# Last pair of a long convolution with spectral mixing: early loads of Z split in two parts and spread over ticks 9 to 14, and two VectorE reflections placed behind the last product

## The chip, the core and the metric

The kernel runs on one core of one Trainium2 chip. A core has a matrix engine (TensorE, PE in the profile; its weight loads are listed as PEld), VectorE (DVE), ScalarE (ACT), GpSimd (POOL) and SyncE (SP), and 16 DMA engines that they share. The metric is the device time of one execution in microseconds (us); the number compared is the median of several runs.

## What is computed

Two steps, one after the other, on x of 8 batches by 5696 positions by 128 channels. The first is a causal convolution of each channel with a filter h as long as the sequence. The second takes the first 64 Fourier modes of that result, mixes the channels of each mode with a complex 128 by 128 matrix, transforms back, adds this to the first result and ends with a dense layer.

```python
Xf = rfft(x, n=2*S, axis=1); Hf = rfft(h, n=2*S, axis=0)
x = irfft(Xf * Hf, n=2*S, axis=1)[:, :S, :]          # long convolution
X = rfft(x, axis=1); Xr, Xi = X[:, :64].real, X[:, :64].imag
Yr = einsum('bmd,mde->bme', Xr, w_r) - einsum('bmd,mde->bme', Xi, w_i)
Yi = einsum('bmd,mde->bme', Xr, w_i) + einsum('bmd,mde->bme', Xi, w_r)
u = x + irfft(Y, n=S, axis=1)                         # Y is zero beyond mode 64
out = u + maximum(u @ w_ch, 0)
```

Everything between the inputs and the output is in float16, with sums in float32.

## The kernel before

**Tiling.** The 5696 positions are split as 89 by 64, so the long transforms become matrix products with constant matrices: F1, M (read in 90 frequency groups k, "As, M" in the profile), W1 and W2. The batches are handled in four pairs (g_ = 0 to 3). For each pair there is a phase that makes As from x (`a_tile`, "F, Xin"), and then a loop of ticks: the 90 groups are cut into 23 ticks of four (the last has two).

**One tick.** `tick(g_, t)` issues, for tick t: `second`, 16 TensorE matmuls of As with M into PSUM; then `products`, which multiplies by the filter's spectrum on VectorE ("U<-Xs,Hs", or "U<-ps,Hs" in every fourth tick, straight from PSUM), in most ticks after ScalarE has copied PSUM to Xs (`copied`). For tick t - 2 it issues `third`: four matmuls of U with W1 and W2, two evacuations by ScalarE into a buffer Zs or Zt, and one store by SP from that buffer to the scratch `zscr` in HBM. For tick t - 3 it issues `modes_of`: eight small matmuls with G that add up the 64 modes in PSUM bank 7. The buffers Zs0 to Zs4 and Zt0 to Zt3 are used in turn; in the last pair there are eight of them (`NZS`), so tick s + 8 writes where tick s has been, and `third(s + 8)` can't start its evacuation before the store of tick s has landed. All ScalarE evacuations and copies stand in one program order.

**After the ticks of the last pair.** The 64 modes of the pair are evacuated to XT in two instructions, the first on ScalarE, the second ("xtn", the negated part) on VectorE behind it, as both read one bank. `mix` multiplies XT with the mode matrices W, `y_out` evacuates that to Y, eight transposes and two evacuations make C. Then the output stage: for each of the 16 chunks of Z (4 pairs by 4 chunks), `u_tile` adds up matmuls of Z with the constants S4a and S4b, which transform back, and of C with the constant IBs, and evacuates to UT on VectorE or ScalarE; `o_tile` applies the dense layer and stores to the output. In both kernels the first U tile's matmuls with Z stand ahead of `mix` on TensorE, and other tiles' stand between the parts of `mix`.

**Loads of the output stage.** A chunk of Z is read back from `zscr` into one of five places ZT0 to ZT4, each in two parts: part a with 128 rows of 8 KB (1024 KB), part b with 52 rows (416 KB) in partitions 32 to 83; partitions 0 to 31 of part b are cleared by a GpSimd memset (`clear_zt`). The places lie on memory that is still in use during the last pair's ticks: ZT2 on the first rows of the filter's spectrum (Hs), ZT0 and ZT1 on the middle and late part of As, S4b on its first part, IBs and S4a on M. So each load waits for the last reader of what it overwrites (`zt_old`). The constants IBs (734.2 KB), S4a (734.2 KB) and S4b (481.9 KB) hold only the first half of their columns; the rest, 2759 columns, is filled by `reflect` (L525), which writes the mirrored columns times a sign per row: S4b on ScalarE (L530), S4a and IBs on VectorE (L532).

**The order around the change** is written out by hand. The dictionary `early` (L540 to 543) says at which tick of the last pair which load is issued. They are issued by GpSimd, whose queue is in order: a waiting load or clear holds up those behind it. `pace` makes each wait for the product of its own tick t on VectorE. In this kernel the order is S4b at tick 6, IBs at 8, both parts of ZT2 at 10, clear of ZT2b at 11, clear of ZT0b at 14, both parts of ZT0 at 15, S4a at 16, ZT1 at 21 (`NT - 2`; this one also waits for the last pair's stores up to tick 14, `SLACK`). Behind the ticks follow WI, ZT3 and ZT4. The later chunks are loaded by SP. VectorE's order behind the ticks is: the last product, "xtn", the reflection of S4a, two Y evacuations, one C evacuation, the reflection of IBs, UT evacuations.

Semaphore waits are derived by a recorder from what each instruction reads and writes; all tiles' instructions are recorded through helpers, so most lines of the profile show L325 (matmul), L313, L315, L317, L319 (evacuations), L322 (DMA) and L611 (products).

Of the kernel before, what the change touches and what calls it, by code (L numbers as in the profile page):

```python
# [4 lines left out]
P = 128  # L5
# [118 lines left out]
def bass_long_conv_fft__then__afno_spectral_mix_kernel(nc, x, h, moe_w_r, moe_w_i, moe_w_ch, out):  # L124
# [8 lines left out]
    NP = B // 2  # L133
# [24 lines left out]
    s4 = np.stack([back[:, None, None] * np.cos(ang), -back[:, None, None] * np.sin(ang)], axis=0)  # L158
    RB, PB = 2 * NK - P, 32
# [13 lines left out]
    ib = modes.copy()  # L173
    ib[:, 0] *= 0.5
    ib = ib.T.reshape(2, M, NQ, J).transpose(1, 0, 3, 2).reshape(P, J, NQ)
# [30 lines left out]
    def at(name, cols, dt, off):  # L206
        return nc.alloc_sbuf_tensor_at(name, [P, cols], dt, offset=off)
# [58 lines left out]
    ib_sb = at("IBs", S, F16, a_mi)  # L266
    s4_sb = [at("S4a", S, F16, a_mi + 2 * S), at("S4b", S, F16, a_as)]
# [26 lines left out]
    def pv(bank, off, dims, p0=0, n=P):  # L294
        return bass.AP(ps, p0 * 4096 + bank * 512 + off, [[4096, n]] + [list(d) for d in dims])
# [5 lines left out]
    def bank(i):  # L301
        return ("bank", i)
# [3 lines left out]
    def evac(dst, src, reads, writes, scale=None, eng=None, after=()):  # L306
        e = eng
        if e is None:
            turn[0] ^= 1
            e = "scalar" if turn[0] else "vector"  # L310
        if e == "scalar":
            if scale is None:
                R.add(e, lambda h_: h_.copy(dst, src), reads, writes, after=after)  # L313
            else:
                R.add(e, lambda h_: h_.activation(dst, src, COPY, scale=scale), reads, writes, after=after)  # L315
        elif scale is None:
            R.add(e, lambda h_: h_.tensor_copy(dst, src), reads, writes, after=after)  # L317
        else:
            R.add(e, lambda h_: h_.tensor_scalar_mul(dst, src, scale), reads, writes, after=after)  # L319

    def dma(eng, dst, src, ring, reads=(), writes=(), after=()):
        R.add(eng, lambda h_: h_.dma_start(dst, src), reads, writes, ring=ring, after=after)  # L322
# [6 lines left out]
    def once(key, toks):  # L329
        if key in first:  # L330
            return []
        first[key] = 1
        return list(toks)
# [77 lines left out]
    def idle(n, b0, m=P):  # L411
        for i in range(n):
            mm(pv(b0 + i % 2, 0, [[2 * NK, 2], [1, 2 * NK]], 0, m), f1_sb[:, 0:m], ap(f1_sb, 2 * NK, 0, P, 0, [[0, 2], [1, 2 * NK]]),
               True, True, [("f1",)], [bank(b0 + i % 2)])
# [7 lines left out]
    for j in range(16):  # L422
        t = turns("h", [0, 2, 4])
        for i in range(8):
            d = 8 * j + i
            for r in range(2):
# [6 lines left out]
             eng="vector" if j % 4 == 1 else "scalar")  # L433
# [6 lines left out]
    def share(n):  # L440
        a, v = load["scalar"] + COST[n][0], load["vector"] + COST[n][1]
        e = "scalar" if a <= v else "vector"
        load[e] = min(a, v)
        return e
# [42 lines left out]
    def load_g(i):  # L487
        s0, s1 = i * GP, min(i * GP + GP, NS)
        dma("sync", g_sb[:, s0 * P:s1 * P], bass.AP(c_g, s0 * P, [[GW, P], [1, (s1 - s0) * P]]), "c", (),
            [("g", i)], after=[("ag", k) for k in range(s0, s1)])  # L490
# [3 lines left out]
    def load_w(i):  # L494
        w = 2 * M * D // NWP
        h_ = i % 2
        dma("gpsimd", w_sb[i // 2][:, h_ * w:(h_ + 1) * w], bass.AP(wd, i * w, [[2 * M * D, P], [1, w]]), "p",
            [t_ for t_ in WD if (t_[1] * M + t_[2]) * D // w == i], [("w", i)], after=[("xc", i // 2)] + pace)
# [4 lines left out]
    M_ALL = [("m", i) for i in range(MP)]  # L503
# [3 lines left out]
    ZX = [("zs", i, b) for i in range(NZ, NZL) for b in range(2)]  # L507
    zt_old = [(AST, AST), (AST, AST), (H_ALL, H_ALL), (H_ALL, H_ALL), (M_ALL[3:6], G_ALL)]

    def load_zt(i, eng="sync", more=()):  # L510
        g_, c_ = divmod(i, J // ZB)
        for part, (p0, r0, n) in enumerate(((0, 0, P), (PB, P, RB))):
            old = list(once(("zt", i % NC, part), zt_old[i % NC][part])) + list(more) + pace
            dma(eng, bass.AP(zt[i % NC][part], p0 * ZP, [[ZP, n], [1, ZP]]),
                bass.AP(zs, (g_ * 2 * NK + r0) * J * 256 + c_ * ZB * 256, [[J * 256, n], [1, ZP]]),
                "q" if eng == "gpsimd" else "t", [("zd", g_, s_) for s_ in range(NT)], [("zt", i % NC, part)], after=old)

    def clear_zt(i):
        z32 = zt[i][1][0:PB, :].bitcast(U32)
        R.add("gpsimd", lambda e: e.memset(z32, 0), (), [("zt0", i)], after=list(zt_old[i][1]) + pace)  # L520

    def load_ib():
        dma("gpsimd", ib_sb[:, 0:SH], c_ib.ap(), "p", (), [("ib", 0)], after=M_ALL[0:2] + pace)

    def reflect(eng, t, n, col, key, after):  # L525
        MN = S - SH
        dst, src = bass.AP(t, SH, [[S, n], [1, MN]]), bass.AP(t, SH - NQ - 1, [[S, n], [-1, MN]])
        sc = sg_sb[0:n, col:col + 1]
        if eng == "scalar":
            R.add(eng, lambda e: e.activation(dst, src, COPY, scale=sc), [key + (0,), ("sg",)], [key + (1,)], after=after)  # L530
        else:
            R.add(eng, lambda e: e.tensor_scalar_mul(dst, src, sc), [key + (0,), ("sg",)], [key + (1,)], after=after)  # L532

    def load_s4(part):
        n = PB + RB if part else P
        dma("gpsimd", s4_sb[part][0:n, 0:SH], bass.AP(c_s4, part * SH, [[2 * SH, n], [1, SH]]), "p", (),
            [("s4", part, 0)], after=pace + (AST if part else M_ALL[1:4]))

    V, A = "vector", "scalar"
    early = {0: lambda: (load_w(6), load_w(7), load_id()),  # L540
             6: lambda: load_s4(1), 8: lambda: load_ib(), 10: lambda: load_zt(2, "gpsimd"), 11: lambda: clear_zt(2),
             14: lambda: clear_zt(0), 15: lambda: load_zt(0, "gpsimd"), 16: lambda: load_s4(0),
             NT - 2: lambda: (load_zt(1, "gpsimd", SLACK), clear_zt(1))}
    w_at = {11: (0, 1), 17: (2, 3), 25: (4, 5)}
    pace = []
    SLACK = [("zd", NP - 1, s_) for s_ in range(NT - NZL)]

    def load_id():
        dma("gpsimd", id_sb[:, :], bass.AP(c_w, 2 * P, [[3 * P, P], [1, P]]), "p", (), [("id",)], after=ZY)
# [135 lines left out]
    for g_ in range(NP):  # L685
        for t in range(NT + LM if g_ + 1 == NP else NT):
            if g_ == 0 and t % 2 == 0 and t // 2 < NG:
                load_g(t // 2)
            tick(g_, t)
            assert g_ + 1 < NP or not wp  # L690
            if g_ == NP - 1 and t in early:
                pace[:] = [("u", min(t, NT - 1) % NU)] if t else []
                early[t]()
        if g_ + 1 < NP:
            load.update(scalar=600.0, vector=0.0)
            third(g_, NT - 2)
            a_tile(0, [0], share(720))
            a_tile(1, [2], share(720))
            third(g_, NT - 1)
            load["scalar"] += 560.0  # L700
            a_tile(2, [0], share(720))
            modes_of(g_, NT - 3)
            a_tile(3, [4], share(720))
            modes_of(g_, NT - 2)
            a_tile(4, [2], share(720))
            modes_of(g_, NT - 1)
            load["scalar"] += 700.0
        evac(bass.AP(xt, 6 * g_ + 2, [[B * XTW, P], [3 * B, M], [2, 2], [1, 2]]), pv(MB, 0, [[1, M], [M, 2], [P, 2]]),
             [bank(MB)], [("xt", g_)], 1.0 / 64, eng="scalar", after=[("ag", k) for k in range(NS + 2 * XN, NK)])
        evac(bass.AP(xt, 6 * g_, [[B * XTW, P], [3 * B, M], [1, 2]]), pv(MB, M, [[1, M], [P, 2]]),  # L710
             [bank(MB)], [("xtn", g_)], -1.0 / 64, eng="vector" if g_ + 1 == NP else "scalar", after=[("ag", k) for k in range(NS + 2 * XN, NK)])
        if g_ + 1 < NP:
            for j in range(5, 32):
                a_tile(j, [(0, 4, 6, 2)[(j - 5) % 4]], "both" if j == 31 else share(720))
                if j == 31:
                    idle(4, 2)
                if wp and j % 2 == 1:
                    dst, src_, ring, tok = wp.pop(0)
                    dma("gpsimd", dst, src_, ring, (), [tok], after=[("as", j)])
                if g_ + 2 == NP:  # L720
                    for i in w_at.get(j, ()):
                        load_w(i)
# [54 lines left out]
             src, [bank(t), bank(t + 1)], [("u_", ub, 2 * c_ + half)], eng=e, after=once(("u", ub), old))  # L777

    XTT = [(n, g_) for g_ in range(NP) for n in ("xt", "xtn")]
    reflect("vector", s4_sb[0], P, 0, ("s4", 0), M_ALL[1:4])  # L780
    reflect("scalar", s4_sb[1], PB + RB, 1, ("s4", 1), AST)
    MQ = M // 4

# [25 lines left out]
    for hb in range(2):  # L809
        evac(c_sb[:, hb * 512:hb * 512 + 512], ps16[:, (6 + hb) * 1024:(6 + hb) * 1024 + 512], [bank(6 + hb)],  # L810
             [("c", hb)], 2.0 * 64 / S, eng="vector" if hb else "scalar", after=WT)
    reflect("vector", ib_sb, P, 2, ("ib",), M_ALL[0:3])


    n_o = [0]
# [52 lines left out]
    for g_ in range(NP):  # L868
        last = g_ == NP - 1
        order = [(c_, b) for b in range(2) for c_ in range(NCH)] if last else [(c_, b) for c_ in range(NCH) for b in range(2)]  # L870
        for n, (c_, b) in enumerate(order):
            i = NCH * g_ + c_
# [44 lines left out]
```

## Time and profile before

| | |
|---|---|
| time, median of 3 runs | 379.2 us (378.95 to 379.32) |
| the profiled execution | 380.74 us, its span 378.9 us |
| PE busy | 358.8 us (95%) |
| ACT busy | 311.2 us (82%) |
| DVE busy | 302.5 us (80%) |
| POOL busy | 83.7 us (22%) |
| mean granted TensorE clock | 0.991 |
| DMA packets | 84560, 103.92 MB, mean 274 GB/s |
| chain that ended last | PE 76%, ACT 11%, DVE 7%, DMA 4% |
| reflection of S4a, of IBs (VectorE, 128x2759) | 2157 ns, 1811 ns |

All times of the trace are counted from the start of the span. The last pair's products run from 213.7 to 252.0 us. A row of a timeline gives the start, the length, the engine, the line, the operation with its output and inputs, how many instructions are merged in it, and in brackets the idle time of the engine before it and what ended that. A row of waits gives who waited for whom, the total in us, the number of times and the longest. In the DMA view, q0 ("software_dynamic") holds what GpSimd issues and q1 ("hardware_dynamic") what SP issues; the time to landing of a DMA is counted from its issue. Matmuls are pipelined and their ends modelled, so a busy PE is not PE at its peak.

### The profile page before, as it was taken

The page shows a single profiled execution, that of the slowest core. Times are in us where ns is not written, and L with a number is a line of the kernel's source. Part 1 is how long each engine was busy: PE and PEld are TensorE (multiplying, and loading weights), DVE is VectorE, ACT ScalarE, POOL GpSimd, SP SyncE. Part 2 cuts the span into 40 slices and gives each one's busy share as a digit, 9 for nine tenths or more (in the row PEclk, how much of TensorE's full clock was granted, in tenths as well). Part 3 has the DMA queues.
Part 4 walks back from the last instruction along what each step waited for, and adds up shares of the span by engine and source line. Part 5 has one row for each costly group of instructions (what it writes and reads, how often), then busy time and mean ns, then how long its engine had stood idle before and what let it go on. Part 6 is the DMA issues. An engine that isn't in the chain of part 4 may idle for free.

```text
span 378.9 us, 11952 instructions
## 1 busy us (share of the span) xinstructions
PE 358.8 (95%) x5107; PEld 275.4 (73%) x5107; DVE 302.5 (80%) x332; ACT 311.2 (82%) x493; POOL 83.7 (22%) x137
## 2 busy tenths in 40 slices
PE   7998989999989999899999899979999999999994
PEld 3897856667856667766668666648898988988872
DVE  7557998998989998889998888754547767777786
ACT  8358989998989998999998899975457677777785
POOL 8500012320932312823305303309000000000000
PEclk9999999999999999999999999998999999999998
DMA  7999599998999996999997989999999999999768
GB/s 138 209 278 349 142 233 231 273 276 233 116 133 234 254 256 162 144 153 238 256 258 122 340 262 290 290 301 331 396 410 365 354 414 406 419 408 379 301 267 348
DMA packets 84560, 103.92 MB, mean 274 GB/s; under 512 B 22126, under 2 KB 68974, under 8 KB 81538
## 3 DMA queue, kind: packets, MB, share of 16 engines
q1 hardware_dynamic: 59643, 67.73, 52.1%
q0 software_dynamic: 24864, 35.43, 44.6%
q8 instruction: 40, 0.66, 0.7%
q14 instruction: 13, 0.11, 0.1%
HBM read 70.61 MB, written 51.12 MB: 321 GB/s over the span
## 4 chain that ended last, share of the span: by engine, by line
PE 76%; ACT 11%; DVE 7%; DMA 4%; issue 1%; DVEq 0%; ACTq 0%
PE ps L325 76%; ACT As L315 7%; DMA zscr<-Zt 4%; DVE As L319 3%; DVE U L603 1%; ACT R L851 1%; ACT UT L313 1%; DVE Hs L317 1%; DVE UT L317 1%; DMA F<-cF 1%; DVE IBs L532 0%; ACT XT L315 0%; DVE O L852 0%; ACT Hs L313 0%; DVE Os L852 0%
## 5 line engine op out<-in xcount | busy, mean ns | idle before, releaser
L325 PE MATMUL ps<-U,Wc 128*128 128x512 f16 (+1 forms) x368 | 94.5, 376 | 2.5 <-ACT Zt L313 2.5
L611 DVE TENSOR_TENSOR U<-Xs,Hs 128x2048 f16<-128x2048 f16 (+1 forms) x68 | 80.5, 1188 | 10.8 <-ACT Xs L313 8.8
L313 ACT CAST Xs<-ps 128x1024 f16<-128x1024 f32 (+1 forms) x72 | 69.5, 971 | 7.0 <-PE ps L325 4.8
L852 DVE TENSOR_TENSOR O<-ps,R 128x512 f32<-128x512 f32 x81 | 52.5, 684 | 19.6 <-ACT R L851 11.2
L313 ACT CAST Zs<-ps 128x512 f16<-128x512 f32 (+1 forms) x120 | 62.9, 603 | 0.0
L851 ACT ACTIVATE R<-ps 128x512 f32<-128x512 f32 x96 | 50.9, 572 | 14.3 <-PE ps L325 13.9
L319 DVE TENSOR_SCALAR As<-ps 128x720 f16<-128x720 f32 (+1 forms) x60 | 49.8, 878 | 7.6 <-PE ps L325 6.7
L315 ACT ACTIVATE As<-ps 128x720 f16<-128x720 f32 (+1 forms) x72 | 51.0, 765 | 5.4 <-PE ps L325 4.4
L325 PE MATMUL ps<-F,Xin 128*128 128x180 f16 x512 | 52.3, 247 | 2.9 <-ACT Ah L315 1.0
L325 PE MATMUL ps<-As,M 64*128 64x128 f16 x1440 | 48.7, 217 | 4.2 <-DVE U L603 3.5
L325 PE MATMUL ps<-WI,UT 128*128 128x256 f16 x360 | 51.8, 279 | 0.5 <-DVE O L852 0.4
L325 PEld LDWEIGHTS ps<-F,Xin 128*128 128x128 f16 x512 | 43.3, 142 | 10.8 <-DVE As L319 3.9
L325 PEld LDWEIGHTS ps<-U,Wc 128*128 128x128 f16 x368 | 28.2, 97 | 31.4 <-ACT Zs L313 5.9
L325 PEld LDWEIGHTS ps<-As,M 64*128 64x128 f16 x1440 | 40.3, 94 | 10.8 <-DVE U L603 4.2
L322 POOL DMA_DIRECT2D Xt<-in_x_dram x48 | 24.9, 522 | 100.8 <-PE ps L325 100.2
L611 DVE TENSOR_TENSOR U<-ps,Hs 128x2048 f16<-128x2048 f32 x20 | 45.7, 2283 | 0.0
L313 ACT CAST UT<-ps 128x712 f16<-128x712 f32 x40 | 30.0, 752 | 17.4 <-PE ps L325 16.4
L325 PEld LDWEIGHTS ps<-WI,UT 128*128 128x128 f16 x360 | 39.3, 152 | 4.2 <-issue 1.9
L325 PE MATMUL ps<-IBs,C 128*128 128x356 f16 x128 | 39.2, 314 | 1.3 <-DVE UT L317 0.6
L313 ACT CAST Zt<-ps 128x512 f16<-128x512 f32 (+1 forms) x64 | 33.7, 599 | 2.6 <-DMA zscr<-Zt 2.5
L325 PEld LDWEIGHTS ps<-G,Zs 128*128 128x128 f16 x468 | 25.6, 96 | 12.1 <-DMA G<-cG 0.3
L325 PE MATMUL ps<-G,Zs 128*128 128x2 f16 (+2 forms) x468 | 28.8, 191 | 0.0
(88 smaller groups left out, 501.4 us busy)
## 6 DMA issues: line engine op xcount, KB each, us to landing
out_dram<-O SPq DMA_DIRECT2D x39, 512.0 KB, 7.3
zscr<-Zs SPq DMA_DIRECT2D x57, 256.0 KB, 5.6
zscr<-Zt SPq DMA_DIRECT2D x31, 256.0 KB, 7.1
Xt<-in_x_dram POOLq DMA_DIRECT2D x24, 320.0 KB, 6.8
W<-wscr POOLq DMA_DIRECT2D x8, 512.0 KB, 9.4
M<-cM POOLq DMA_DIRECT2D x5, 720.0 KB, 20.9
ZT0a<-zscr SPq DMA_DIRECT2D x3, 1024.0 KB, 9.2
Xr<-in_x_dram POOLq DMA_DIRECT2D x8, 320.0 KB, 14.5
```

What stands on the lines that cost most here:

```text
L313: R.add(e, lambda h_: h_.copy(dst, src), reads, writes, after=after)
L315: R.add(e, lambda h_: h_.activation(dst, src, COPY, scale=scale), reads, writes, after=after)
L317: R.add(e, lambda h_: h_.tensor_copy(dst, src), reads, writes, after=after)
L319: R.add(e, lambda h_: h_.tensor_scalar_mul(dst, src, scale), reads, writes, after=after)
L322: R.add(eng, lambda h_: h_.dma_start(dst, src), reads, writes, ring=ring, after=after)
L325: R.add("tensor", lambda h_: h_.matmul(o, l, r, start=st, stop=sp), reads, writes)
L603: R.add("vector", lambda e, b=b, s_=s_: e.tensor_tensor(bass.AP(u_s[i], b * 512, [[2048, P], [1024, 2], [1, n * D]]), s_, hv, MULT), [tok, ...
L611: R.add("vector", lambda e: e.tensor_tensor(uv, src, hv, MULT), bk + [("h", t, 0), ("h", t, 1, 0), ("h", t, 1, J)], [("u", i)])
L851: R.add("scalar", lambda e: e.activation(rv, src_r, RELU), bk, [("r", i % NR)], after=once(("r", i % NR), G_ALL + XTT + [("y", q) for q in ...
L852: R.add("vector", lambda e: e.tensor_tensor(ov, src_u, rv, ADD), bk + [("r", i % NR)], [key + (h_,)], after=once(key, old))
```

## The change

It has two parts. The function `load_zt` gets an argument that picks which of the two parts of a chunk to load, and the early loads stand in another order: part a of ZT2 at tick 9; the clear of ZT2b and part a of ZT0 at tick 10; part b of ZT2 at tick 12; the clear of ZT0b and part b of ZT0 at tick 14. S4b (6), IBs (8), S4a (16) and ZT1 (21) stay at their ticks. And the two reflections on VectorE are moved from behind the ticks and from behind C to the place between the ticks of the last pair and the evacuations of XT, IBs first, so that on VectorE they follow the last product and precede "xtn". No instruction is added or removed, and no byte more or less is moved.

```diff
-    def load_zt(i, eng="sync", more=()):
+    def load_zt(i, eng="sync", more=(), parts=(0, 1)):
         g_, c_ = divmod(i, J // ZB)
-        for part, (p0, r0, n) in enumerate(((0, 0, P), (PB, P, RB))):
+        for part in parts:
+            p0, r0, n = ((0, 0, P), (PB, P, RB))[part]
...
     early = {0: lambda: (load_w(6), load_w(7), load_id()),
-             6: lambda: load_s4(1), 8: lambda: load_ib(), 10: lambda: load_zt(2, "gpsimd"), 11: lambda: clear_zt(2),
-             14: lambda: clear_zt(0), 15: lambda: load_zt(0, "gpsimd"), 16: lambda: load_s4(0),
+             6: lambda: load_s4(1), 8: lambda: load_ib(), 9: lambda: load_zt(2, "gpsimd", (), (0,)),
+             10: lambda: (clear_zt(2), load_zt(0, "gpsimd", (), (0,))), 12: lambda: load_zt(2, "gpsimd", (), (1,)),
+             14: lambda: (clear_zt(0), load_zt(0, "gpsimd", (), (1,))), 16: lambda: load_s4(0),
              NT - 2: lambda: (load_zt(1, "gpsimd", SLACK), clear_zt(1))}
...
+        if g_ + 1 == NP:
+            reflect("vector", ib_sb, P, 2, ("ib",), M_ALL[0:3])
+            reflect("vector", s4_sb[0], P, 0, ("s4", 0), M_ALL[1:4])
         evac(bass.AP(xt, 6 * g_ + 2, [[B * XTW, P], [3 * B, M], [2, 2], [1, 2]]), pv(MB, 0, [[1, M], [M, 2], [P, 2]]),
...
     XTT = [(n, g_) for g_ in range(NP) for n in ("xt", "xtn")]
-    reflect("vector", s4_sb[0], P, 0, ("s4", 0), M_ALL[1:4])
     reflect("scalar", s4_sb[1], PB + RB, 1, ("s4", 1), AST)
...
-    reflect("vector", ib_sb, P, 2, ("ib",), M_ALL[0:3])
```

## The prediction

> **What bounds the kernel now.** I read the page's busy rows first: TensorE (PE) 358.8 of 378.9 us, ScalarE (ACT) 311.2, VectorE (DVE) 302.5. That is a mean over unlike stages, and the change touches one stage only: the last pair's ticks (about 214 to 257 us) and the mixing behind them (to 267 us). So next comes the chain of waits cut to 254 to 268 us, in order of time; a row is start, length, what.
>
> ```profile
> 240.65 13.97 DMA zscr<-Zt
> ...
> 254.71 0.59 ACT Zt L313
> ...
> 264.47 0.42 DVE C L319
> 264.89 1.73 DVE IBs L532
> 266.62 0.81 DVE UT L317
> 267.43 0.04 issue
> 267.48 0.53 PE ps L325 x5
> ```
>
> Two places carry the change. At 254.71 ScalarE empties tick 21 into Zt, whose buffer still holds tick 13 (eight buffers in the last pair); tick 13's store, issued at 240.65, needed 13.97 us. At 264.89 the reflection of IBs stands between the evacuation of C and the first evacuation of UT. The waits of 250 to 268 us price both, and show idle time on VectorE between them:
>
> ```profile
> DVE XT L319 <- ACT XT L315: 5.2, 1, 5.2
> ...
> ACT Zt L313 <- DMA zscr<-Zt: 2.5, 1, 2.5
> PE ps L325 <- ACT Zt L313: 2.5, 1, 2.5
> ...
> PE ps L325 <- DVE UT L317: 0.6, 1, 0.6
> ```
>
> The timelines of ScalarE, then of VectorE, around that place (start, length, instruction, idle before it):
>
> ```profile
> 246.55 2.06 ACT L313 CAST Zs<-ps 128x512 f16<-128x512 f32 x4
> ...
> 254.71 1.63 ACT L313 CAST Zt<-ps 128x512 f16<-128x512 f32 x4 [2.52 <-DMA zscr<-Zt]
> 256.74 0.38 ACT L315 ACTIVATE XT<-ps 128x256 f16<-128x256 f32 x1 [0.41 <-PE ps L325]
> ```
> ```profile
> 251.31 0.69 DVE L611 TENSOR_TENSOR U<-Xs,Hs 128x1024 f16<-128x1024 f16 x1 [0.24 <-ACT Xs L313]
> 257.23 0.29 DVE L319 TENSOR_SCALAR XT<-ps 128x128 f16<-128x128 f32 x1 [5.23 <-ACT XT L315]
> 257.44 2.16 DVE L532 TENSOR_SCALAR S4a<-S4a,SG 128x2759 f16<-128x2759 f16 x1
> ```
>
> Before 252 us the ticks run at ScalarE's pace: 9.78 of 10.00 us busy from 240 to 250. Last, the DMA queues in three stretches, 235 to 239, 240 to 243 and 245 to 250 us. q0 carries GpSimd's (POOL's) loads, q1 the stores that SP issues; columns are packets, MB (of a million bytes), share of the engines.
>
> ```profile
> q0 software_dynamic: 147, 1.00, 83.7%
> q1 hardware_dynamic: 352, 0.17, 14.5%
> ```
> ```profile
> q1 hardware_dynamic: 1354, 0.67, 74.5%
> q0 software_dynamic: 37, 0.22, 17.6%
> ```
> ```profile
> q0 software_dynamic: 228, 1.43, 91.8%
> q1 hardware_dynamic: 128, 0.07, 4.3%
> ```
>
> The reader is to see that a store (512 packets of 512 bytes) gets 352/4 = 88 or 128/5 = 26 packets a microsecond while loads flow, and 1354/3 = 451 when they pause. So stores come home between loads: issued at 233.65, 234.63, 236.79 and 238.69 (ticks 9 to 12) they landed 10.2, 9.9, 8.5 and 7.3 us later, all from 243.85 to 246.0, behind Z2's second part (232.82 + 10.6 = 243.4); tick 13's landed at 254.65, behind S4a (242.80 + 11.5 = 254.3). The DMA share is near 1 throughout.
>
> **The change, part by part.**
>
> *Issue times.* Each load waits for its tick's product and POOL's order. Products 9, 10, 12, 14, 16 end at 230.05, 232.0, 235.3, 239.0, 242.3, and POOL issued Z2a 0.3 us behind product 10. So Z2a goes out at 230.3 (was 232.30), the clear of Z2b fills 232.1 to 233.9 (1.80 by its row), Z0a follows at 233.9 (was 241.75), Z2b at 235.6 (was 232.82), Z0b behind the other clear at 240.95 (was 242.28), S4a at 242.6 (was 242.80). Four load issues in both, 0.53 us each, and both clears: POOL pays nothing, and SP's queue gets no new issue. What counts is that 1024 KB (Z0a) moves from behind the stores of ticks 9 to 12 to in front of them.
>
> *Stores.* A load's packets start about 2.1 us behind its issue (IBs: issued at 228.87, packets from 231). IBs, then Z2a, Z0a and Z2b (0.75 + 2.52 MB) now form one stream from 231: each is queued before the one ahead is through. At the 1.00/4 = 0.25 MB/us of 235 to 239, or the 0.286 of 245 to 250, it lasts 13.1 or 11.4 us, to 244.1 or 242.4. Z0b (ready at 243) and S4a (244.7), 1.18 MB, carry on to 248.8 or 247.1. The pause in which ticks 9 to 12 landed is gone. By 231, q1 had moved 3592 packets since 216, the stores of ticks 0 to 6. In the next 16 to 17.8 us it gets 26 to 88 a microsecond: 0.8 to 3.0 stores, at the mean of the two windows (57) about 1.9. So tick 7 comes through and tick 8 or tick 9 is the first that is stuck until the loads end. S4a landed 1.4 us behind its last packets (about 252.9), and the next store 0.35 behind that: the stuck store lands at 248.9 to 250.5, the later ones every 0.76 (as after 254.65).
>
> Who waits: ScalarE's evacuation of tick 16 (buffer of tick 8) at 244.56, or of tick 17 (tick 9) at 246.55; behind it on ScalarE stand the copies Xs, so VectorE's products and TensorE follow. From there to the XT evacuation at 256.74, without the 2.52 us stall, are 9.66 and 7.66 us of ScalarE-paced work. XT then starts at 258.6 to 260.2 (tick 8) or 256.6 to 258.2 (tick 9): +1.9 to +3.5, or -0.1 to +1.5. I take +1.6, between the two, as 1.9 stores leave tick 8 at the edge. The old stall is in this number: by then tick 13's store (5 x 0.76 behind tick 8's) is no longer late. Ends: tick 10 stuck first, -1.3; tick 7, +5.3.
>
> *Reflections.* Behind the last product (end 252.0) VectorE sat idle 5.23 us, of which 2.52 are the stall. Without a stall there, the second XT evacuation is due at 257.23 - 2.52 = 254.71. The two reflections need 1.81 (IBs, by its row) + 2.16 = 3.97 us: VectorE is free at 255.97, so the XT evacuation is 1.26 late, and all mixing matmuls wait for it, and TensorE has only the 16 matmuls of the first U tile to put ahead of it in both kernels. Cost +1.26; bounds 0 (the stall stays, and covers them) and +1.26. S4a has landed by then. In return UT's first evacuation no longer stands behind IBs: the 0.55 us wait of TensorE at 267.48 goes, -0.55; the next evacuations, 1.47 us early or more by VectorE's idle rows, hide.
>
> *Clock.* The stall cost more than itself: from 256.2 to 259.6 the granted clock was 0.51, and 32 mixing matmuls took 1.73 us (257.69 to 259.42), the next 32 0.93. Over 3.4 us that is some 1.6 us. In the changed kernel this leaves the mixing, but a wait of 1.6 + 2.5 = 4.1 us inside the ticks, where TensorE is busy all of each window too, brings one like it: 0, with bounds of -1.6 and +1.6.
>
> **Sum:** +1.6 + 1.26 - 0.55 + 0 = +2.3 us. The profiled execution took 380.74 us, a span of 378.9 and 1.84 around it; it would become 383.0. The median of the runs is 379.2, 1.54 lower, so 381.5.
>
> **Rivals.**
> **B, faster: the stores get through.** If loads and stores shared the engines evenly, or the loads ran above some 0.30 MB/us, the first stream would end by 241.8 and leave a pause ahead of Z0b in which ticks 8 to 10 land in time; tick 13's store then meets only Z0b and S4a, 1.18 MB instead of 2.2, and lands before 252.2. The stall goes: -2.52 - 0.55 + 1.26, and with it the cold clock, up to -1.6: 375.8 to 377.4. The point of decision is tick 9's store home by 246.55. For it: 0.317 MB/us between 259 and 262 us (0.95 MB in 3 us). Against it: 0.25 in the very stretch in which Z2 is loaded now. The Trainium skill, "DMA: Bandwidth & Descriptors", section "Queues, rings and completion order", says that a DMA engine takes turns between queues packet by packet, a packet holding some 9 to 17 descriptors; by that the stores would keep a good share and B would be the outcome. The trace speaks against it: 0.56 to 2.4 store packets per load packet, while a load's are up to 8 KB and a store's 512 bytes. On the clock, the same skill, "TensorE: Matmul & The Clock Gate", section "Why this matters for your kernels", warns of idle gaps over some 3 us; by it a 2.5 us gap would cost no clock, and B would give 377.4. Here the gap of 2.45 us was followed by 0.51.
> **C, no change: only the place in the queue changes.** All loads and the stores up to tick 13 are the same work on full engines. If ticks 7 to 12 just make it, tick 13 lands at 254.65 as now, the reflections hide in the 5.23 us, and only 0.55 is won: 378.7. Against it: tick 9 has 246.55 - 243.85 = 2.7 us to spare, and Z0a alone takes 1.05/0.286 = 3.7.
> **D, the loads aren't spread.** Were Z0a held at tick 10 by TensorE's reads of As, the burst would stay: 378.7, or up to 379.9 with the reflections exposed. POOL's rows speak against it: its waits end with products or 0.8 us behind.
>
> **Chances.** Forecast 0.57, B 0.20, C 0.13, D 0.10. About 0.2% (0.76 us) is what a measurement of this kernel can tell from no change. Slower: 0.52 of the forecast and 0.05 of D, 0.57. Same: 0.05 of the forecast (tick 9 or 10 stuck late), 0.10 of C, 0.05 of D, 0.20. Faster: B and 0.03 of C, 0.23. The range goes from B's upper end, 377.4, to 384.6: tick 8 stuck to the end (+3.5 + 1.26 - 0.55) and most of a second cold stretch.
>
> **What would show it.** Right: an idle row on ScalarE before a Zs evacuation of tick 16 or 17, ended by a zscr store; no such row before Zt at tick 21; q1 under 100 packets a microsecond from 234 to 247; the XT evacuation on VectorE right behind a reflection, with TensorE idle before the first mixing matmul; no idle TensorE before UT. Wrong: stores of ticks 8 to 10 landing within 12 us, or loads faster than 0.30 MB/us.

## The result, and the profile after

The changed kernel took 378.0 us (median of 22 runs, 375.88 to 378.95), the kernel before on the same occasions 379.29 us (377.38 to 381.74): a ratio of 0.9964, 95% interval 0.9946 to 0.9982. So it is faster, by some 1.4 us (0.4%), where +2.3 us was forecast; a second measurement gave 0.9968 (0.9941 to 0.9995). The two profiled executions are 380.74 us before (span 378.9) and 378.95 after (span 377.2); both lie at the slow end of their kernel's runs.

The chain of waits of the changed kernel, 252 to 268 us, no longer holds a DMA or the reflection of IBs:

```profile
252.00 1.93 PE ps L325 x24
...
260.74 0.61 ACT C L315
261.35 0.05 issue
261.40 6.64 PE ps L325 x106
```

Of its waits from 250 to 268 us this is left; there is no row of ScalarE waiting for a store, and none of TensorE waiting for UT:

```profile
DVE XT L319 <- ACT XT L315: 0.9, 1, 0.9
```

The timelines of ScalarE, of VectorE and of POOL at that place:

```profile
252.20 1.70 ACT L313 CAST Zt<-ps 128x512 f16<-128x512 f32 x4
254.25 0.39 ACT L315 ACTIVATE XT<-ps 128x256 f16<-128x256 f32 x1 [0.35 <-PE ps L325]
```
```profile
252.10 0.94 DVE L533 TENSOR_SCALAR IBs<-IBs,SG 128x2759 f16<-128x2759 f16 x1
252.95 0.94 DVE L533 TENSOR_SCALAR S4a<-S4a,SG 128x2759 f16<-128x2759 f16 x1
254.74 0.29 DVE L319 TENSOR_SCALAR XT<-ps 128x128 f16<-128x128 f32 x1 [0.85 <-ACT XT L315]
```
```profile
253.13 2.49 POOL L521 MEMSET ZT1b<- 32x2048 uint32 x1
```

Tick 21's evacuation starts at 252.20 instead of 254.71. Each reflection takes 0.94 us where it took 1.81 and 2.16, and VectorE even waits 0.85 us for its XT evacuation. The two evacuations of C come at 260.74 on ScalarE and 260.99 on VectorE (264.21 and 264.47 before): 3.5 us are won up to there. Of these 2.5 are the stall. The other 1.0, between the XT and the C evacuation on VectorE (6.25 us instead of 7.24), goes with the clock, which is 1.00 from 252 to 262 us where 0.51 was granted from 256.2 to 259.6. Two stretches of 3.4 us show it, first before, then after; the columns are the busy times of PE, PEld, DVE, ACT and POOL with the number of instructions, the TensorE clock, the DMA share and the GB/s:

```profile
256.20:259.60 3.40, 3.38 (x55) 3.21 (x56) 2.37 (x2) 2.97 (x3) 3.40 (x4) 0.51 1.10 300
```
```profile
255.00:258.40 3.40, 3.27 (x105) 3.30 (x106) 0.46 (x2) 2.53 (x2) 3.40 (x6) 1.00 1.00 341
```

Not all of that reaches the end. The last instruction on an engine ends 3.35 us earlier (371.95 against 375.30), the span only 1.7. From there to the end of the span, while the last output stores land, it is 5.2 us instead of 3.6: the store of 364.19 took 4.8 us to land, its counterpart before (367.54) 2.8. Over all the kernels profiled here this tail is 3.6 to 5.4 us; it is 3.6 in only two, the kernel before and one of those with the reflections alone. Both have the old loads, but two more profiles with exactly these loads have 5.11 and 5.25, so the loads alone don't decide it; whether they bear on it, and why the tail differs, stays open. The last view here is that of the tick stretch, 231 to 247 us, with the same columns, first the kernel before, then the changed one:

```profile
231.00:247.00 16.00, 16.00 (x260) 10.51 (x254) 13.55 (x10) 15.78 (x26) 6.25 (x7) 1.00 0.97 298
```
```profile
231.00:247.00 16.00, 16.00 (x265) 10.68 (x260) 13.55 (x10) 15.78 (x26) 5.69 (x7) 1.00 1.03 354
```

The share is about 1 in both, yet the second moved 354/298, a fifth more. Part of that is that more of the loads lie in this stretch after the change (3.96 MB of them against 3.11).

### The profile page after: what moved, and what is told of

Read it like the earlier page. It is cut to its first block, busy times and chain, and to the rows that moved or that the text cites. A ratio compares the mean times of both kernels' runs of the same rounds, so it can differ in the third digit from the quotient of the medians.

```text
span 377.2 us, 11950 instructions
## 1 busy us (share of the span) xinstructions
PE 357.9 (95%) x5107; PEld 275.3 (73%) x5107; DVE 300.9 (80%) x332; ACT 311.2 (83%) x493; POOL 84.6 (22%) x137
## 4 chain that ended last, share of the span: by engine, by line
PE 81%; ACT 11%; DVE 6%; issue 1%; DMA 0%; DVEq 0%
PE ps L325 80%; ACT As L315 7%; DVE As L319 2%; DVE U L605 1%; ACT R L854 1%; ACT UT L313 1%; DVE Hs L317 1%; DMA F<-cF 0%; DVE UT L317 0%; ACT XT L315 0%; DVE O L855 0%; ACT Hs L313 0%; DVE Os L855 0%; ACT Ah L315 0%; DVEq L105 0%
## 5 line engine op out<-in xcount | busy, mean ns | idle before, releaser
L325 PE MATMUL ps<-F,Xin 128*128 128x180 f16 x512 | 53.7, 252 | 2.9 <-ACT Ah L315 1.0
L325 PEld LDWEIGHTS ps<-F,Xin 128*128 128x128 f16 x512 | 44.8, 143 | 10.6 <-DVE As L319 3.4
L317 DVE CAST UT<-ps 128x712 f16<-128x712 f32 x24 | 21.4, 892 | 9.5 <-PE ps L325 9.5
```

What stands on the lines that cost most here:

```text
L325: R.add("tensor", lambda h_: h_.matmul(o, l, r, start=st, stop=sp), reads, writes)
```

## The experiments

The theories. **L**: the burst of loads at tick 15 and 16 stood in front of the stores of ticks 13 and 14, and spreading the loads takes it away. **R**: the reflections bring the gain. **N**: the stall belongs to the DMA speed of that one execution. **M**: a reflection on VectorE and a GpSimd memset exclude each other. And the prediction's own: stores of ticks 8 and 9 starve.

**Each kernel once more, unchanged.**

> The kernel before once more, unchanged, to see what of its trace repeats. Theory L (the spread loads take the burst away from in front of tick 13's store): the burst is in the program, so the stall of ScalarE before tick 21's evacuation repeats at 1.5 to 3 us, with tick 13's store at 12 to 15 us to landing. Theory N (the speed of the DMA engines in that one execution made it): IBs and S4b, which took 7.3 and 6.4 us to land before and 5.5 and 5.2 after with nothing changed ahead of them, land faster here too, and the stall is under 1 us or absent. Both: the reflections on VectorE take 2.16 and 1.81 us again, each beside a GpSimd memset.

> The changed kernel once more, unchanged. Theory L: no stall at tick 21 again, tick 13's store home within 10 us. Theory N: a stall at ticks 16, 17 or 21 may show when the loads run at 0.25 MB/us. Theory M (a VectorE reflection and a GpSimd memset exclude each other): both reflections at 0.94 us again, and the memset of ZT1b longer than 1.83 us. The idle spell of the DMA engines at 367 us and the long landings of the last output stores: gone if they were chance.

One profiled execution each, 379.38 and 380.2 us. The kernel before, in its waits from 240 to 256 us:

```profile
ACT Zt L313 <- DMA zscr<-Zt: 0.8, 1, 0.8
```

Here tick 13's store landed in time, at 246.2, and tick 14's was late. With the two profiles of the reflections alone, below, which have the same loads, the stall is 2.5, 0.8, 0 and 0 us, in executions of 380.74, 379.38, 377.69 and 377.69 us: the stall differs between executions, as N says, and the two without it lie below the median of their kernel (one is the shortest of its 12 runs). N's own sign did not come: IBs and S4b took 7.2 and 6.2 us to land, about as before. The 231 to 247 us stretch ran at 333 GB/s here, not 298. The reflections were 2.43 us (S4a, beside a memset) and 0.93 (IBs, which ended before the memset of ZT4b began); TensorE did not wait for UT. The changed kernel, its waits from 240 to 256:

```profile
ACT Zs L313 <- DMA zscr<-Zs: 0.7, 1, 0.7
```

That is the prediction's mechanism, small: the stores of ticks 8 and 11 took 13.0 and 13.6 us to land, and tick 11's (at 250.5) held up tick 19's evacuation. In the other five profiles of kernels with exactly these loads there is no stall. The tail was 5.4 us here, so the long landings of the last output stores came again.

**The loads alone, the reflections alone.** The first kernel keeps the new `early` and has both `reflect("vector", ...)` lines at their old places; the second keeps the old `early` and `load_zt` and has both at the new place.

> Only the loads are spread; both reflections stand where they were. Theory L: the whole gain but that of the reflections, -0.7 to -1.5 us against the kernel before; no stall before tick 21; the reflection of IBs at 1.8 us again in front of the first UT evacuation, TensorE idle some 0.55 us there. Rival R (the reflections bring the gain): within 0.3 us of before. The prediction's theory (stores starved at ticks 8 and 9): slower by 0.5 us or more.

> The loads alone, a second sample, since the first (-0.9 us) had an interval that reached zero. Theory L: -0.7 to -1.2 us. In the trace no stall over 0.7 us, and TensorE idle 0.5 to 0.9 us before UT wherever the memset of ZT4b stands beside the reflection of IBs, none where it doesn't.

> Only the reflections are moved; the loads are those of before. Theory L: -0.5 us (the wait of TensorE for UT behind IBs), as the stall at tick 21 stays and hides both reflections. Rival R: -1.0 to -1.5 us, the measured gain of the whole change. The prediction's theory: 0 to -0.5, reflections hidden in the stall. Theory M: both reflections take 0.94 us, as no memset runs between 252 and 254 us, against 2.16 and 1.81 in the kernel before.

> The reflections alone, a second sample (first: -0.3 us, interval to both sides of zero). Theory L: -0.2 to -0.6 us; the stall at tick 21 or 22 is anything from 0 to 2.5 us in the trace, as in the kernel before, and whatever it is, the reflections take 0.94 us each and are done before the second XT evacuation is due.

> The changed kernel on the same chip as the two half changes below, so that the three can be compared. -1.0 to -1.6 us against before, as in its first measurement. Theory M: both reflections at 0.94 us. Stall of ScalarE between ticks 16 and 22: 0 to 0.7 us.

Twelve runs each. The loads alone: 0.9975 (0.9944 to 1.0006) and 0.9983 (0.9958 to 1.0007). The reflections alone: 0.9991 (0.9960 to 1.0023) and 0.9985 (0.9957 to 1.0013). The whole change beside the second of each: 0.9968 (0.9941 to 0.9995). Every half's interval reaches 1, so neither is shown by its time. The middles multiply to the whole (0.9979 x 0.9988 = 0.9967), two thirds of it to the loads; that is as far as times go. The traces say more. With the loads alone there is no stall in either profile; with the reflections alone both take 0.93 to 0.94 us and TensorE is never idle before UT, as in every kernel that has them there. With the reflections at the old place TensorE waited 0.81 us before UT in the first profile, 0.32 in the second. In that second one (VectorE, then POOL):

```profile
255.09 0.94 DVE L533 TENSOR_SCALAR S4a<-S4a,SG 128x2759 f16<-128x2759 f16 x1
...
261.48 1.59 DVE L533 TENSOR_SCALAR IBs<-IBs,SG 128x2759 f16<-128x2759 f16 x1
```
```profile
253.47 1.82 POOL L521 MEMSET ZT1b<- 32x2048 uint32 x1
...
260.49 1.84 POOL L521 MEMSET ZT4b<- 32x2048 uint32 x1
```

S4a met no memset (253.47 + 1.82 = 255.29 is its tail) and took 0.94. IBs met one that ended at 262.33 and itself ended at 263.07, 0.74 behind it. In the kernel before (POOL, then the reflection of IBs on VectorE):

```profile
257.03 1.83 POOL L520 MEMSET ZT1b<- 32x2048 uint32 x1
...
264.06 1.82 POOL L520 MEMSET ZT4b<- 32x2048 uint32 x1
```
```profile
264.81 1.81 DVE L532 TENSOR_SCALAR IBs<-IBs,SG 128x2759 f16<-128x2759 f16 x1
```

There the memsets ended at 257.03 + 1.83 = 258.86 and 264.06 + 1.82 = 265.88, the reflections at 259.60 (S4a) and 266.62 (IBs): 0.74 behind, both times. TensorE's wait for UT follows: in the five profiles with the reflections at the old place IBs took 2.08, 1.90, 1.81, 1.59 and 0.93 us, and TensorE waited 0.81, 0.63, 0.55, 0.32 and 0 (the 1.90 is from the kernel with more in the burst, below).

**The clear of ZT1b put first**, so that its memset runs beside the reflections.

```diff
-             NT - 2: lambda: (load_zt(1, "gpsimd", SLACK), clear_zt(1))}
+             NT - 2: lambda: (clear_zt(1), load_zt(1, "gpsimd", SLACK))}
```

> The changed kernel with the clear of ZT1b in front of ZT1's loads instead of behind them, so that the GpSimd memset runs from about 251.3 to 253.1 us, when VectorE comes to the first reflection (252.1). Theory M (reflection and memset exclude each other, whoever is first goes on): the IBs reflection takes until 0.75 us behind the memset's end, 1.5 to 2.0 us in place of 0.94, S4a still 0.94, VectorE reaches the second XT evacuation with under 0.3 us idle or late, and TensorE waits up to 0.5 us for it. Rival (2.16 and 1.81 in the kernel before came from something else, such as the running DMAs): both stay at 0.94 and XT keeps its 0.85 us of idle.

One execution, 378.78 us. VectorE, then POOL:

```profile
251.49 1.80 DVE L533 TENSOR_SCALAR IBs<-IBs,SG 128x2759 f16<-128x2759 f16 x1
253.21 0.92 DVE L533 TENSOR_SCALAR S4a<-S4a,SG 128x2759 f16<-128x2759 f16 x1
254.13 0.29 DVE L319 TENSOR_SCALAR XT<-ps 128x128 f16<-128x128 f32 x1
```
```profile
250.76 1.80 POOL L521 MEMSET ZT1b<- 32x2048 uint32 x1 [8.01 <-DVE U L613]
```

The memset ended at 252.56, IBs at 253.29, 0.73 later; S4a at 0.92; the 0.85 us of idle ahead of XT is gone. M stands, and whoever started first went on: in the changed kernel it is the memset that came second and took 2.49 us instead of 1.8. The Trainium skill, "SBUF — State Buffer", section "Who interferes with whom", says that VectorE in certain fast modes and GpSimd share one pair of ports that the first holds for its whole instruction; this trace agrees in each of the cases above.

**More load traffic in front, the changed kernel; more in the burst, the kernel before.** Two loads of W, 1 MB together, that were issued at tick 0:

```diff
-    early = {0: lambda: (load_w(6), load_w(7), load_id()),
+    early = {0: lambda: load_id(),
...
+             10: lambda: (clear_zt(2), load_zt(0, "gpsimd", (), (0,)), load_w(6), load_w(7)), 12: ...
```

> The changed kernel with two loads of W (512 KB each) taken from tick 0 and put behind Z0a at tick 10: double the traffic that the change put in front of the stores of ticks 8 to 12. The prediction's mechanism (stores starve while loads flow, and a store stuck early holds up ScalarE's whole order): the stores of ticks 8 to 10 land 2.5 to 3.5 us later than in the changed kernel (from 246 us on), ScalarE stands 1.5 to 3 us before an evacuation of tick 16 or 17, and the time rises by 1.5 to 3 us over the changed kernel, that is +0.3 to +1.7 us over before. Rival (engines shared evenly enough): stall under 0.5 us, time as the changed kernel.

In the second kernel they follow `load_zt(0, "gpsimd")` at tick 15.

> The kernel before with the same two loads of W put behind Z0 at tick 15, in the late burst, in front of S4a. Theory L (the burst in front of the stores of ticks 13 and 14 sets the stall at ticks 21 and 22): those stores land 2.5 to 3.5 us later, the stall grows by about that from its 0 to 2.5 us, the second XT evacuation comes 2.5 to 3.5 us later, and the time rises by 2 to 4 us over before. Theory N (the stall is chance): no clear change.

The first: 1.0071 (1.0031 to 1.0111) of before, ten runs; that is, by the two ratios, some 4 us over the changed kernel, more than the 1.5 to 3 expected. Its waits from 240 to 262 us, and the stretch of 249.2 to 252.6 (columns as above):

```profile
ACT Zs L313 <- DMA zscr<-Zs: 3.1, 1, 3.1
```
```profile
249.20:252.60 3.40, 2.41 (x28) 1.75 (x30) 0.00 (x0) 2.15 (x4) 0.00 (x0) 0.50 1.09 328
```

Tick 9's store took 16.0 us and landed at 249.5, tick 17's evacuation stood 3.09 us, and the clock stood at 0.50 for 6.8 us: the picture that the prediction drew for the change itself, at twice its dose. This is also the run that moved most in 231 to 247 us, 385 GB/s at a DMA share of 1.03. The second: 1.0080 (1.0047 to 1.0112); tick 14's store landed at 255.2, the stall before tick 22 was 2.3 us, and the clock fell to 0.50 behind a TensorE gap of 2.33 us. Beside the 0.8 us in the kernel before at its median time (379.38 us) the stall grew by 1.5 us, less than the 2.5 to 3.5 expected. L holds: what stands in front of a store decides, at either place.

**Less in front.** All of ZT2, and then Z2b alone, moved behind WI (`load_zt(2, "gpsimd")` at the head of the loop over ZT3 and ZT4; `load_zt(2, "gpsimd", (), (1,))` ahead of it):

> The changed kernel with both loads of ZT2 taken out of the ticks and put behind WI, ahead of ZT3 (the clear of ZT2b stays): 1440 KB less in front of the stores. Theory L: the stores of ticks 8 to 14 land within 8 us, no stall of ScalarE between ticks 16 and 22 in any profile, and time equal to the changed kernel or up to 0.5 us better. The risk is behind the ticks: ZT2 is needed at about 267.5, ZT3 at 271.5, ZT4 at 275.5; each load of 1440 KB takes some 4 to 4.5 us, so they would land at about 266, 270.5 and 275. If the chunks that SP reloads slow them, TensorE waits there and the time is 1 to 3 us worse.

> The changed kernel with Z2b (416 KB) alone moved behind WI, ahead of ZT3, half way between the changed kernel and the one with all of ZT2 late, where ZT4b landed at 277.4 and TensorE waited 2.2 us for it from 275.3. Expected: ZT4b lands 1.2 to 2 us later than in the changed kernel (272.7), at 274 to 274.7, so no wait; the stores of ticks 8 to 12 land up to 1 us earlier; time equal to the changed kernel within 0.3 us, or 0.3 us better where that one stalls at all. If ZT4b lands behind 275.3, worse by that.

The first cost 1.0107 (1.0057 to 1.0158; six runs). No stall in the ticks, as L says, but the waits from 255 to 290 us show where it came back:

```profile
PE ps L325 <- DMA ZT4b<-zscr: 2.2, 1, 2.2
```

ZT4b landed at 277.4, 2.2 us late. Its profiled execution was its shortest (380.2 against a median of 382.85), so the wait was probably longer in the others; no trace shows that. The second gave 0.9986 (0.9962 to 1.0011): ZT4b at 273.7, no stall and no wait anywhere, and nothing gained on the change. No version here is shown to beat the changed kernel.

## Why the prediction was wrong, point by point

*Issue times*: right. POOL issued Z2a at 230.52, Z0a 233.99, Z2b 235.81, Z0b 241.06 and S4a 242.82, all within 0.25 us.

*Stores*: the mechanism was right, its size was the step that failed: the term was +1.6 us, and in the changed kernel no store held up ScalarE (0.7 us in one of six profiles with these loads). The second XT evacuation came 2.5 us earlier, where this term and that of the reflections had it 2.9 later. The text gave the stores 26 to 88 packets a microsecond, 57 in the mean, beside loads of 0.25 to 0.286 MB/us, in a stream without a pause up to 247.1 or 248.8. The loads' mean came out at the upper end of that, 3.17 MB from 231 to 242 us or 0.288 MB/us. But they did not flow evenly. The changed kernel's DMA view, 237 to 238.9 us, then 239 to 241.8, then 242 to 245:

```profile
q1 hardware_dynamic: 599, 0.30, 52.6%
q0 software_dynamic: 63, 0.39, 49.9%
```
```profile
q0 software_dynamic: 162, 1.08, 91.6%
q1 hardware_dynamic: 199, 0.10, 11.8%
```
```profile
q1 hardware_dynamic: 1646, 0.82, 90.6%
q0 software_dynamic: 46, 0.15, 22.8%
```

While the loads ran at 1.08/2.8 = 0.39 MB/us the stores got 199/2.8 = 71 packets a microsecond, as forecast; in a dip of the loads to 0.39/1.9 = 0.21 they got 599/1.9 = 315. Over the whole of 231 to 242 us they got 1587 packets, 144 a microsecond (132 to 178 in the six profiles with these loads). From 242 to 245 a pause of 1646 packets, 3.2 stores, opened ahead of Z0b, whose packets came some 3.5 us behind its issue and not 2.1. Why the loads dip, and why Z0b came late, no run shows. In the second profile of the changed kernel Z0b's packets came 2.0 us behind its issue, the stores got 973 packets from 242 to 245, and there tick 11's store was late. Tick 8's store did slip, to 242.7 (10.8 us against 6.3), and stayed 2 us ahead of its need.

So the store rate failed because it was read from stretches in which loads flowed all the time and carried over to a longer one in which they did not. A second profile alone would not have mended it: in the same two stretches of the kernel before, repeated, the stores got 73 and 46 packets a microsecond, 59 in the mean, much as in the first. The loads had 0.30 and 0.33 MB/us there, so their 0.25 and 0.286 belonged to one execution. And the engines were taken for full, because "the DMA share is near 1 throughout". With the old loads a share of 0.97, 1.01, 1.03 and 1.02 went with 298, 333, 332 and 324 GB/s, and with more loads in the stretch 1.03 went with 354 and with 385: the share didn't tell how much the engines could still take. So rival C's premise of full engines isn't borne out either.

*The old stall*: counted as a fixed 2.52 us. It was 2.5, 0.8, 0 and 0 in four executions with the old loads.

*Reflections*: +1.26 forecast, 0 measured. The row that mis-sized it is 1.81 and 2.16: both had a memset beside them in the profile of POOL, and without it each is 0.94, 1.88 together, which fits in front of an XT evacuation that starts 2.6 us behind the last product (252.18 to 254.74). In the kernel with more load traffic in front one of them met a memset at the new place (IBs 2.46, S4a 0.92 us), and VectorE came to XT without any idle. So the reasoning on the order holds; the durations failed.

*UT behind IBs*: -0.55 forecast; the wait went, in every kernel with the reflections moved. It is 0.8 to 0 us at the old place, by where the memset of ZT4b falls.

*Clock*: forecast 0 with bounds of 1.6 either way. Between the two profiles it was -1.0, as no gap of TensorE replaced the old one in the ticks.

*Rival B* named what happened, with the right point of decision (a pause ahead of Z0b, and tick 9's store home by 246.55; it came at 244.2), and gave 375.8 to 377.4. The measured 378.0 is near that partly by luck: B holds the +1.26 that did not come, and takes off a stall of 2.52 us that was smaller in the three other executions with the old loads. The longer tail behind the last instruction may have its part; the times without a profile don't show it.

## What to carry to other kernels

A queue's rate read from a stretch of heavy traffic on another queue does not hold for a longer stretch with gaps in that traffic: count the packets over all of it. Take a second profile of the same kernel before a stall of a few microseconds is counted as fixed, and don't read a DMA share of 1 as a full engine; compare GB/s. Before an instruction's duration is moved with it to another place, look at what the other engines did beside it, here GpSimd's memsets beside a VectorE scaling from SBUF to SBUF. And a store that must be home before its buffer is written again has slack that can be listed (landing against the evacuation eight ticks on): loads can be moved in front of it until that is used up, here 1 MB (with 0.7 us of stall in one profile of six) and not 2.

## What was not expected of the hardware

A reflection of 128x2759 on VectorE takes 0.94 us alone and ends 0.73 to 0.74 us behind the end of a GpSimd memset that was there first. On TensorE's clock the runs give no simple rule. TensorE gaps of 2.33 and 2.45 us were each followed by a granted clock of 0.50 for 3.41 us, and during a gap of 3.06 us it fell to 0.50 and stayed there for 6.83; a gap of 2.23 us (the wait for ZT4b in the kernel with all of ZT2 late) was followed by 1.00, as were the gaps of 0.84 and 0.87 us. And three executions, the changed kernel's first profile among them (29.17 to 32.58 us), had 3.41 us at 0.50 early on, with no gap over 0.95 us in the 10 us before.
